# Batch 0's output product by fewer multiplications: four of its six row tiles as two pairs, and the work beside them in a new order

## The chip, the core and the metric

The kernel runs on one core of a Trainium2 chip. The core has a matrix engine (TensorE, in the profile PE, with its weight loads shown apart as PEld), a vector engine (VectorE, DVE), a scalar engine for functions and copies (ScalarE, ACT), GpSimd (POOL) and SyncE (SP); the last two issue DMA transfers here. The engines run beside each other and wait for each other through semaphores. Matrix products are summed in PSUM, a small memory of eight banks; all other tiles lie in SBUF. The metric is the device time of one execution in microseconds (us), as the median of several runs; smaller is better.

## The reference

An attention over 4 batches, 8 heads, 768 positions of 64 numbers is followed by a two-layer feed-forward block. A query sees the keys nearer than 16 positions, and for each block of 32 keys one summary: the maximum of the keys, the mean of the values.

```python
k_sum = k.reshape(B, H, nb, block, D).max(axis=3)
v_sum = v.reshape(B, H, nb, block, D).mean(axis=3)
scores_l = scale * np.matmul(q, k.transpose(0, 1, 3, 2))
mask_l = np.abs(pos[:, None] - pos[None, :]) < window
scores_s = scale * np.einsum('bhsd,bhnd->bhsn', q, k_sum) + np.log(block)
scores_all = np.concatenate([np.where(mask_l, scores_l, -1e9), scores_s], axis=-1)
a = softmax(scores_all)                      # the last axis
x = np.matmul(a, np.concatenate([v, v_sum], axis=2))
x = x.transpose(0, 2, 1, 3).reshape(B * S, H * D)     # 3072 x 512
h = x @ w_in                                 # 512 x 2048
out = (h / (1.0 + np.exp(-1.702 * h))) @ w_out        # 2048 x 512, f32
```

## The kernel before

Each batch has 768 tokens, worked on in two halves of 384. For each half the attention makes x, transposed, in `xTT`; the input stage (`ff_in`, `ff_open`, `ff_one`) multiplies it by `w_in` in 16 tiles of 128 features (four matmuls of 384 columns each) and ACT writes the activated result to `gTb`, which holds 16 feature tiles by 768 tokens. The output stage multiplies `gTb` by `w_out` into rows of 128 tokens, six per batch. The attention of the next half or batch runs beside the input and output stages of the one before.

The output product is done in one of two ways:

- plainly (`ff_out`, line 869): 16 matmuls of 512 columns for a row tile of 128 tokens, in four parts of four; then ACT copies the tile from PSUM and SP stores it;
- as a pair by seven products (`product`, line 775; Strassen's scheme in Winograd's form): the rows are a pair of token tiles, the features two halves of eight tiles, the columns two halves of 256. Seven products of eight matmuls of 256 columns replace two plain tiles. They take raw tiles of `gTb` and `w_out`, four sums of `gTb` (`gs`, by `g_sums` on DVE) and four differences of `w_out` (`ws`, by `w_sum`, each in two parts). Products 1, 6, 7 and 4 add up in one bank (A), 5 and 3 in another (B), 2 in a third (C). Between them the partial sum in A is saved to `s1` and `s2`, that in B to `s5`, by `keep_it`, and DVE adds them back in `give`; the next product must not write the bank before that copy has read it.

Batch 0 is worked plainly in two units of three tiles; batches 1 to 3 by seven products, with a tile of the first half paired with one of the second. The weight differences are made beside batch 0: four of the eight half differences after the first unit, four in the second unit's input stage.

What sets the order is written out by hand. Every engine runs its instructions in program order (`_Ordered`, line 18). `plan0`, `plan1` and `plan` (lines 1030 to 1038) say which piece of attention follows which block or product: "s" scores of a pair of heads (matmuls into PSUM, then an exponential on ACT), "m" its mask on DVE, "v" the values of two pairs (matmuls, then a reciprocal and a multiplication on DVE for each pair, the norm), "x" the turn of x on PE and its copy, "d" the same by DMA, "q" and "t" turns of queries, "g" a load of ACT's activation table. Two digits are half and pair (or group of two pairs), one digit the pair or group alone. `todo` (line 1102) lists the same for the second unit's input stage: `tk` turns a pair of keys, ACT copies it, DVE takes the block maxima, and POOL makes the halo and summary columns (`rest_k`, line 578). `value_rows` (line 1076) does the values' part: DMAs on SP that copy halo rows, 48 small matmuls that sum blocks (`vsum`, line 280), five DVE instructions that write the sums (`block_sums`), and two DMAs on SP that spread them.

PSUM is cut into two pools: `pmm` has four buffers of one bank, `psb` two buffers of two banks. Scores, values of batches 0, 2 and 3 and the turned x take `psb`; input tiles and output tiles take `pmm`. A new tile waits until some buffer's last reader is done.

POOL issues the loads of q, k and v, which also convert to 16 bits (`load_turned`, `load_v`: twelve loads for a batch's v). They are in POOL's program order together with its copies of keys; `load_batch(1)` stands at line 1027, `load_batch(2)` in the second output stage. For batch 3, waits on POOL (through `gate2`) hold back some loads until transposes by DMA have landed.

## Time and profile before

| | |
|---|---|
| median of 3 runs (range) | 206.83 us (205.51 to 206.84) |
| the profiled execution: time, span | 205.39 us, 203.4 us |
| PE busy, share of the span | 196.7 us, 97% |
| DVE busy | 141.2 us, 69% |
| ACT busy | 125.4 us, 62% |
| POOL busy | 89.9 us, 44% |
| first unit's output stage (batch 0) | from 30.66 us, 14.17 us long |
| second unit's input stage | from 44.83 us, 12.40 us long |
| block sums, then second unit's output stage | from 57.23 us, to 74.46 us |

The span runs from the first to the last record of the trace; the execution's time is longer by its start and end. The busy time of an engine other than PE counts where PE waits for it. Places in time are given from the span's start.

### The profile page before, as it was taken

Reading aid. Unit: us, or ns where it says so; the run is one execution under the profiler, and the core shown is the slowest. Engines: PE = TensorE matmul, PEld = TensorE weight load, DVE = VectorE, ACT = ScalarE, POOL = GpSimd, SP = SyncE. Lnnn points to the kernel's source line nnn. Section 1 sums busy time; section 2 is a strip of 40 time slices with the busy share of each in tenths; the row PEclk is TensorE's granted clock in tenths of the full one; section 3 lists DMA queues with packets and bytes.
Section 4 is the critical chain, followed back from the end, with each engine's and each line's share of the span. In section 5 each row is a group of like instructions: output and inputs, shape, how many; then the busy total and the mean of one; then the engine's idle time right before and its main releaser. Section 6 shows DMA issues by size and latency. Waiting matters only on the chain.

```text
span 203.4 us, 5851 instructions
## 1 busy us (share of the span) xinstructions
PE 196.7 (97%) x2358; PEld 136.6 (67%) x2358; DVE 141.2 (69%) x391; ACT 125.4 (62%) x240; POOL 89.9 (44%) x141
## 2 busy tenths in 40 slices
PE   6889999999999999999999999999999999999993
PEld 5548655556754566655888876666888865578882
DVE  6586894694856884898767789896769567758221
ACT  4584976638786717777871446778670559984220
POOL 7964489447899584000986034000000009980000
PEclk9999999999999999999999999999999999999999
DMA  5999999999999999999999979999022930000223
GB/s 171 169 165 204 207 207 215 189 156 243 116 122 170 176 170 178 127 165 155 114 181 156 173 140 139 110 247 179 0 104 62 185 119 3 0 0 0 106 105 103
DMA packets 95994, 28.13 MB, mean 138 GB/s; under 512 B 83664, under 2 KB 93152, under 8 KB 95968
## 3 DMA queue, kind: packets, MB, share of 16 engines
q0 software_dynamic: 69648, 13.24, 84.8%
q1 hardware_dynamic: 26176, 14.39, 34.8%
q8 instruction: 18, 0.29, 0.6%
q10 hardware_dynamic: 144, 0.13, 0.2%
q14 instruction: 8, 0.07, 0.1%
HBM read 27.26 MB, written 6.29 MB: 165 GB/s over the span
## 4 chain that ended last, share of the span: by engine, by line
PE 91%; DMA 3%; DVE 3%; issue 1%; ACT 0%; POOLq 0%; DVEq 0%
PE ph L28 32%; PE poA L28 16%; PE po L28 11%; PE poB L28 7%; PE phA L28 4%; PE ps_av L28 4%; PE poC L28 4%; PE ps_s L28 3%; DMA qe<-in_q_dram 3%; DVE ks L28 2%; PE ps_t L28 1%; PE ps_x L28 1%; PE phC L28 1%; PE phB L28 1%; PE phE L28 1%; DVE qT L28 1%
## 5 line engine op out<-in xcount | busy, mean ns | idle before, releaser
L28 PE MATMUL ph<-xT,w_in_sb 128*128 128x384 f16 x400 | 67.8, 326 | 0.1
L28 PEld LDWEIGHTS <-w_in_sb 128*128 128x128 f16 x442 | 42.7, 98 | 27.2 <-issue 0.2
L28 ACT ACTIVATE gT<-ph 128x384 f16<-128x384 f32 x100 | 47.9, 491 | 18.4 <-PE ph L28 17.6
L28 PEld LDWEIGHTS <-gT 128*128 128x128 f16 x312 | 28.8, 98 | 11.3 <-issue 0.2
L28 ACT ACTIVATE a_sb<-ps_s 128x768 bf16<-128x768 f32 (+1 forms) x32 | 25.0, 826 | 12.0 <-PE ps_s L28 12.0
L28 PEld LDWEIGHTS <-gs 128*128 128x128 f16 x288 | 27.7, 98 | 3.4
L28 POOL DMA_DIRECT2D vw<-in_v_dram x36 | 24.6, 699 | 11.9 <-DMA kb<-in_k_dram 5.4
L28 POOL TENSOR_TENSOR gs<-gT 128x384 f16<-128x384 f16 x8 | 7.3, 911 | 43.3 <-ACT gT L28 43.2
L28 PE MATMUL po<-w_out_sb,gT 128*128 128x512 f16 x96 | 23.6, 380 | 0.0
L28 PE MATMUL poA<-ws,gs 128*128 128x256 f16 x144 | 18.7, 273 | 0.0
L28 DVE TENSOR_TENSOR a_sb<-a_sb,mk 128x768 bf16<-128x768 bf16 x28 | 14.9, 554 | 5.5 <-ACT a_sb L28 5.0
L28 DVE TENSOR_TENSOR x<-ps_av,rc 128x384 f16<-128x384 f32 x32 | 17.8, 557 | 1.1
L28 DVE TENSOR_TENSOR gs<-gT 128x384 f16<-128x384 f16 (+1 forms) x34 | 13.3, 390 | 7.2 <-ACT gT L28 6.9
L28 POOL DMA_DIRECT2D qb<-in_q_dram x16 | 15.1, 961 | 2.5 <-DMA w_in_sb<-in_moe_w_in_dram 1.2
L28 PEld LDWEIGHTS <-kx 64*128 64x128 bf16 (+1 forms) x378 | 9.9, 95 | 6.8 <-issue 3.6
L28 POOL DMA_DIRECT2D kb<-in_k_dram x14 | 13.6, 986 | 0.3 <-issue 0.3
L28 DVE TENSOR_REDUCE ks<-kx 128x24 bf16<-128x768 bf16 x12 | 11.4, 948 | 3.4 <-ACT kx L28 3.2
L28 ACT ACT_TABLE_LOAD x10 | 12.8, 1283 | 1.0 <-PEq L1240 0.8
L28 ACT ACTIVATE osb<-poA 128x256 f32<-128x256 f32 x9 | 3.5, 384 | 16.1 <-PE poA L28 16.1
L28 ACT ACTIVATE s<-poA 128x256 f32<-128x256 f32 x11 | 4.2, 385 | 11.2 <-PE poA L28 11.2
L28 PEld LDWEIGHTS <-a_sb 128*64 128x64 bf16 (+2 forms) x400 | 7.9, 108 | 2.8 <-issue 1.3
L28 PE MATMUL poA<-ws,gT 128*128 128x256 f16 x72 | 9.3, 273 | 0.0
(117 smaller groups left out, 288.2 us busy)
## 6 DMA issues: line engine op xcount, KB each, us to landing
out_dram<-osb SPq DMA_DIRECT2D x22, 256.0 KB, 3.9
kb<-in_k_dram POOLq DMA_DIRECT2D x14, 192.0 KB, 6.6
qb<-in_q_dram POOLq DMA_DIRECT2D x12, 192.0 KB, 10.5
vw<-in_v_dram POOLq DMA_DIRECT2D x36, 64.0 KB, 5.5
w_out_sb<-in_moe_w_out_dram POOLq DMA_DIRECT2D x4, 512.0 KB, 12.8
w_in_sb<-in_moe_w_in_dram POOLq DMA_DIRECT2D x3, 512.0 KB, 12.4
vw<-vs SPq DMA_DIRECT2D x6, 198.0 KB, 6.6
gT<-in_k_dram SPq DMA_DIRECT2D x2, 384.0 KB, 3.4
```

The source lines that it names most:

```text
L28: r = f(*a, **kw)
```

## The change

Batch 0 is no longer two units of three plain tiles. The first two tiles of the first half are done plainly, and the other four (the first half's last tile and the three of the second half) are two pairs of neighbours, each by seven products, in the order `seq0`. `g_sums0` makes the four sums of `gTb` for them: the first four feature pairs in the second input stage, the other four beside the first products. All weight differences are therefore due by then: one moves into the first output stage (`"w0"`), seven follow it.

The attention beside these stages has new places. `plan0` now spreads batch 0's second half over eight blocks. `plan1` places batch 1's attention over fourteen products. In `values`, a mask can be put between the two norms of a group (`between`), and the values of batch 1 take `psb` but for the first group. The turned x of batches 0 and 1 is copied by ACT and not DVE, for batch 1 (but for the last two) from a `pmm` buffer; two query turns take `psb`. The block sums (`value_rows`) of batch 1 move from the end of the input stage to behind the first product, those of batches 2 and 3 from the second step of the input stage to the last, and always use `pmm`. `xq` of batch 3 moves from step 4 to step 2, and the block sums of batch 0 (`vrows0`) from the thirteenth input tile to the tenth.

Loads: of batch 1's v seven are issued first, the other five in two pieces between the key turns, and the second group of q after them (before, all v, then that group). Batch 2 loads k, q, v and not k, v, q. Batch 3 loads q with k and v after the gate (before, the other way round). The copy that saves `s1`, `s2` and `s5` of the first pair is ACT's for batch 0 and stays DVE's for batches 1 and 2.

```diff
@@ -129,12 +129,11 @@
                 pool.dma_start(out=t2[g][:, :, :, hh].rearrange("p i a d -> p (i a) d"),
                                in_=x[b, h0:h0 + 2].rearrange("h (a p) d -> p (h a) d", p=128))
-    def load_v(b):
+    def load_v(b, pieces=slice(0, 2 * NJ)):
         w5 = vw[b % 2].rearrange("p (j e) h c -> p j e h c", e=2)
         src = v[b].rearrange("h (j e p) d -> e j p h d", e=2, p=64)
-        for j in range(NJ):
-            for e in range(2):
-                pool.dma_start(out=w5[e * 64:e * 64 + 64, j, e, :, 0:D], in_=src[e, j])
+        for j, e in [(j, e) for j in range(NJ) for e in range(2)][pieces]:
+            pool.dma_start(out=w5[e * 64:e * 64 + 64, j, e, :, 0:D], in_=src[e, j])
     FAR = -30000.0
@@ -249,11 +248,9 @@
         load_turned(k, b, kb2, "kb")
         if b == 3:
             pool.tensor_copy(out=gate2, in_=qTs[0][:, NP - 1, 0:1])
+        load_turned(q, b, qb2, "qb", (0,) if b == 1 else (0, 1))
         if b == 1:
-            load_turned(q, b, qb2, "qb", (0,))
-        load_v(b)
-        if b < 3:
-            load_turned(q, b, qb2, "qb", (1,) if b == 1 else (0, 1))
+            load_v(b, slice(0, 7))
     def load_w_in(n0, n1):
         wi = moe_w_in.rearrange("(ko ki) n -> ki ko n", ki=128)
@@ -279,11 +276,7 @@
     def vsum(s):
-        if s == 1 and not vs_ps[0]:
-            ps = [pmm.tile([128, 512], F32, name="ps_vs", tag="mm") for e in range(2)]
-        else:
-            big = psb.tile([128, 1024], F32, name="ps_vs", tag="big")
-            ps = [big[:, 0:512], big[:, 512:1024]]
+        ps = [pmm.tile([128, 512], F32, name="ps_vs", tag="mm") for e in range(2)]
         vs_ps[0] = ps
         w5 = vw[s].rearrange("p (j e) h c -> p j e h c", e=2)
         for j in range(NJ):
...
@@ -598,9 +592,9 @@
         dve.tensor_mul(a, a, mk[:, half * TH:(half + 1) * TH, :].unsqueeze(1)
                        .to_broadcast([128, 2, TH, QT]))
-    def values(b, half, g):
-
-        if b == 1:
+    def values(b, half, g, mm=False, between=()):
+
+        if mm:
             banks = [pmm.tile([128, 512], F32, name="ps_av", tag="mm") for i in range(2)]
         else:
             ps = psb.tile([128, 1024], F32, name="ps_av", tag="big")
@@ -621,6 +615,8 @@
         x2[g] = attp.tile([128, 2, JH, 2, D], F16, name="x2", tag="x2", bufs=4)
         for i in range(2):
             norm(x2[g][:, :, :, i].rearrange("p h j d -> p j h d") if b else x2[g][:, i], pvs[i])
+            for f in between[i:i + 1]:
+                f()
     def norm(x, pv):
         rc = attp.tile([128, 2, JH, 1], F32, name="rc", tag="rc")
@@ -628,13 +624,13 @@
         dve.tensor_mul(x.rearrange("p j h d -> p h j d"), pv[..., 0:D],
                        rc.to_broadcast([128, 2, JH, D]))
-    def tx(half, g):
-        ps = psb.tile([128, 2, HALF], F16, name="ps_x", tag="big")
+    def tx(half, g, eng=dve, mm=False):
+        ps = (pmm if mm else psb).tile([128, 2, HALF], F16, name="ps_x", tag="mm" if mm else "big")
         for i in range(2):
             for j in range(JH):
                 pe.transpose(out=ps[:, i, j * 128:(j + 1) * 128],
                              in_=x2[g][:, i, j].rearrange("p h d -> p (h d)"), identity=ident16)
-        dve.tensor_copy(out=xTT[half][g], in_=ps)
+        copy(eng, xTT[half][g], ps)
     def dx(half, g):
         sp.dma_start(out=xTT[half][g].rearrange("p i (j c) -> p (i j) c", c=128),
@@ -688,6 +684,19 @@
             a, b_, op = {0: (a1[:, r], a2[:, r], ALU.add), 1: (gs[:, 0, j], a1[:, l], ALU.subtract),
                          2: (a1[:, l], a1[:, r], ALU.subtract), 3: (a2[:, l], gs[:, 1, j], ALU.subtract)}[w]
             eng.tensor_tensor(out=gs[:, w, j], in0=a, in1=b_, op=op)
+
+    def g_sums0(j0, j1, which, eng=dve):
+
+        def pairs(n0):
+            a = gTb[:, n0 + j0:n0 + j1, HALF - 128:S].rearrange("p j (a i c) -> p j a i c", i=2, c=128)
+            return a[:, :, :, 0], a[:, :, :, 1]
+
+        (l1, r1), (l2, r2) = pairs(0), pairs(NT // 2)
+        o = [gs[:, w, j0:j1, 0:256].rearrange("p j (a c) -> p j a c", c=128) for w in range(4)]
+        for w in which:
+            a, b_, op = {0: (r1, r2, ALU.add), 1: (o[0], l1, ALU.subtract),
+                         2: (l1, r1, ALU.subtract), 3: (l2, o[1], ALU.subtract)}[w]
+            eng.tensor_tensor(out=o[w], in0=a, in1=b_, op=op)
     N1 = d_model // 2
...
@@ -801,7 +810,7 @@
                 t_ = now[t, name] = spare[:, 2 * HALF + t * N1:2 * HALF + (t + 1) * N1]
             else:
                 t_ = now[t, name] = snap.tile([128, N1], F32, name=name, tag=name)
-            copy(dve if t == 0 and b + 1 < B else act, t_, po)
+            copy(dve if t == 0 and 0 < b and b + 1 < B else act, t_, po)
         def give(o, cols, name):
             if (t, o) not in now:
...
@@ -1027,11 +1039,12 @@
     load_batch(1)
-    plan0 = {1: ["q0", "q1", "q2"], 2: ["s0", "s1", "q3", "m0", "m1"], 4: ["s2", "s3", "m2", "m3"], 6: ["v0", "v1"], 8: ["x0"], 9: ["x1"]}
-
-    plan1 = {-1: ["s00", "s01"], 1: ["t2", "m00", "m01"], 2: ["t3", "s02"], 3: ["s03", "m02"], 4: ["m03", "s10"],
-             5: ["s11", "m10"], 6: ["v00", "m11", "s12", "s13"], 7: ["v01", "g"], 8: ["m12", "m13"],
-             9: ["x00", "x01", "v10"], 10: ["v11"], 11: ["x10"]}
+    plan0 = {0: ["q0", "q1"], 1: ["q2", "q3", "s0", "s1"], 3: ["s2", "s3", "m0", "m1", "w0", "m2", "v0"],
+             5: ["v1", "x0"], 7: ["x1"]}
+
+    plan1 = {0: ["R"], 2: ["s00", "s01"], 4: ["t2", "t3", "m00", "m01"], 5: ["s10", "s11"],
+             6: ["m10", "m11"], 7: ["s02", "s03"], 8: ["m02", "m03"], 9: ["s12", "s13"],
+             10: ["m12", "v00", "g"], 11: ["v01"], 12: ["x00", "v10"], 13: ["x01", "v11"]}
     plan = {-1: ["s00", "s01"], 2: ["m00", "m01"], 3: ["s02", "s03"], 5: ["m02", "m03", "s10", "s11"],
             7: ["m10", "m11", "s12", "s13"], 9: ["m12", "m13"], 10: ["v00", "v01"], 11: ["d00"],
@@ -1048,16 +1061,18 @@
                     gelu_soon()
             elif what[0] == "m":
                 mask(1, i)
+            elif what[0] == "w":
+                w_sum(0, 0)
             elif what[0] == "v":
-                values(0, 1, i)
+                values(0, 1, i, False, (lambda: mask(1, 3),) if i == 0 else ())
             else:
-                tx(1, i)
+                tx(1, i, act)
     def beside(b, slot):
         for what in (plan1 if b == 1 else plan).get(slot, ()):
             half, i = int(what[1:2] or 0), int(what[-1:] if len(what) > 1 else 0)
             if what[0] == "t":
-                tq(i, 1, dve)
+                tq(i, 1, dve, True)
             elif what[0] == "m":
                 mask(half, i)
             elif what[0] == "g":
...
@@ -1092,31 +1108,42 @@
     ws = keep.tile([128, 4, NT // 2, N1], F16, name="ws")
     exp_soon()
     beside0(-1)
-    for i, (ms, part) in enumerate((ms, part) for part in range(4) for ms in range(JH)):
+    for i, (ms, part) in enumerate((ms, part) for part in range(4) for ms in range(2)):
         ff_out(0, ms, part)
         beside0(i)
-        if i in (10, 11):
-            w_sum(i - 10, 0)
-            w_sum(i - 10, 1)
-
-    todo = {3: [lambda: tk(0, 1, act)], 4: [lambda: w_sum(2, 0)], 5: [lambda: tk(1, 1, act)],
-            6: [lambda: w_sum(2, 1)], 7: [lambda: w_sum(3, 0)], 8: [lambda: tk(2, 1, act)], 
-            10: [lambda: w_sum(3, 1)], 9: [lambda: tq(0, 1, dve)], 11: [lambda: tk(3, 1, act)], 12: [lambda: tq(1, 1, dve)],
-            15: [lambda: value_rows(1)]}
-    ff_in(1, range(3))
-    for nt in range(3, NT):
-        ff_in(1, (nt,))
-        for f in todo.get(nt, ()):
+    for what, part in ((0, 1), (1, 0), (1, 1), (2, 0), (2, 1), (3, 0), (3, 1)):
+        w_sum(what, part)
+
+    todo = {3: [lambda: tk(0, 1, act), lambda: load_v(1, slice(7, 9))],
+            5: [lambda: tk(1, 1, act), lambda: load_v(1, slice(9, 2 * NJ))],
+            8: [lambda: g_sums0(0, 4, (0, 1)), lambda: tk(2, 1, act)],
+            9: [lambda: tq(0, 1, dve), lambda: load_turned(q, 1, qb2, "qb", (1,)), lambda: g_sums0(0, 4, (2,))],
+            11: [lambda: tk(3, 1, act)],
+            12: [lambda: tq(1, 1, dve), lambda: g_sums0(0, 4, (3,))]}
+    ff_in(1, order2[0:4])
+    for f in todo[3]:
+        f()
+    for n in range(4, NT):
+        ff_in(1, (order2[n],))
+        for f in todo.get(n, ()):
             f()
     exp_soon()
-    beside(1, -1)
-    for i, (ms, part) in enumerate((ms, part) for ms in range(JH) for part in range(4)):
-        ff_out(1, ms, part)
+    for i, (t, what) in enumerate(seq0):
+        product(0, t, what)
+        if i == 0:
+            g_sums0(4, NT // 2, (0,))
+        if i == 1:
+            g_sums0(4, NT // 2, (2, 3))
         beside(1, i)
+        if i == 0:
+            g_sums0(4, NT // 2, (1,))
         if i == 2:
-            load_batch(2)
-        if i in (9, 11):
-            xk(i // 2 - 4, 0)
+            load_turned(k, 2, kb2, "kb")
+        if i == 4:
+            load_turned(q, 2, qb2, "qb")
+            load_v(2)
+        if i in (10, 12):
+            xk(i // 2 - 5, 0)
     halves[0] = True
@@ -1128,7 +1155,11 @@
                 win_sum(w)
         for n in range(0, NT, 2):
             if n == 0:
-                ff_open(order2[0:4], (lambda: tx(1, 1)) if b == 1 else None)
+                ff_open(order2[0:4], (lambda: tx(1, 0, act)) if b == 1 else None)
+                if b == 1:
+                    tx(1, 1)
+                    for nt in order2[4:6]:
+                        ff_one(0, nt)
             elif n == 2:
                 for nt in order2[0:4]:
                     ff_one(1, nt)
@@ -1136,16 +1167,16 @@
                 g_sums(1)
             else:
                 for nt in order2[n:n + 2]:
-                    for half in range(2):
+                    for half in range(int(b == 1 and n == 4), 2):
                         ff_one(half, nt)
                 g_sums(n // 2, dve, (0, 1) if n + 2 == NT else (0, 1, 2, 3))
             if nxt:
                 if n == 0 and b > 1:
                     pool.tensor_copy(out=gate2, in_=xTT[1][1][:, 1, 0:1])
-                    load_turned(q, b + 1, qb2, "qb")
-                if n // 2 == 1:
+                    load_v(b + 1)
+                if n // 2 == 7:
                     value_rows(s)
-                if n // 2 == 2 * b:
+                if n // 2 == 2:
                     xq(0, s)
                     xq(1, s)
                 if n // 2 in (2, 3, 4, 5):
```

Left out are the buffers of `tq` and the token rows that `product` reads and stores for a pair (for batch 0 the tiles at 256 and 384, or 512 and 640).

More of the change, by code (lines that the diff above doesn't have):

```diff
@@ L560, in tk, with tq @@
         rest_k(p, s, pool)
-    def tq(p, s, eng):
-        ps = pmm.tile([128, 1024], BF16, name="ps_t", tag="mm")[:, 0:S]
+    def tq(p, s, eng, big=False):
+        ps = (psb.tile([128, 2048], BF16, name="ps_t", tag="big") if big
+              else pmm.tile([128, 1024], BF16, name="ps_t", tag="mm"))[:, 0:S]
         turn_tiles(ps, qb2[p // 2][:, p % 2], NJ)
@@ L827, in product @@
             if last:
-                store("o1", t * 128, lo)
+                store("o1", tok_l, lo)
         elif what == 6:
@@ L1069, in beside @@
             elif what[0] == "v":
-                values(b, half, i)
+                first_ = b == 1 and half == i == 0
+                values(b, half, i, first_, (lambda: mask(1, 3),) if first_ else ())
             elif what[0] == "d":
@@ L1073, in beside @@
             else:
-                tx(half, i)
+                tx(half, i, act, True)
     def value_rows(s):
@@ L1085 @@
         ff_in(0, (nt,))
-        if nt == 12:
+        if nt == 9:
             act.activation(out=gate3[:, 0:1], in_=gate[:, 0:1], func=ACT.Copy)
```

14 lines of the change are left out of this document (8 added, 6 removed).

## The prediction

> **What bounds the kernel now.** The page's busy times come first, then its shares of the chain that ended last.
>
> ```profile
> PE 196.7 (97%) x2358; PEld 136.6 (67%) x2358; DVE 141.2 (69%) x391; ACT 125.4 (62%) x240; POOL 89.9 (44%) x141
> ...
> PE 91%; DMA 3%; DVE 3%; issue 1%; ACT 0%; POOLq 0%; DVEq 0%
> ```
>
> PE is on the chain nine tenths of the time. Who PE itself waited for, and for how long (total, times, longest):
>
> ```profile
> PE ps_h L28 <- DVE warm L28: 1.3, 1, 1.3
> PE ps_q L28 <- DMA qe<-in_q_dram: 0.8, 1, 0.8
> PE ps_b L28 <- DVE ks L28: 0.8, 2, 0.4
> PE ps_k L28 <- ACT kb L28: 0.5, 1, 0.5
> ```
>
> All of these belong to the opening attention. Three stages carry the change: the output stage of batch 0's first half (30.66 to 44.83), the input stage of its second half, and the second output stage with batch 1's attention. Columns are PE, weight loads, DVE, ACT, POOL, clock, DMA.
>
> ```profile
> 30.66:44.83 14.17, 14.17 (x183) 7.42 (x181) 9.16 (x21) 7.68 (x11) 9.18 (x12) 1.00 1.80 188
> 44.83:57.23 12.40, 12.40 (x108) 8.14 (x114) 8.40 (x13) 10.12 (x20) 9.67 (x21) 1.00 1.94 175
> 57.23:74.46 17.23, 17.23 (x316) 9.68 (x316) 12.40 (x32) 10.60 (x15) 14.03 (x23) 1.00 1.79 160
> ```
>
> PE is busy in every microsecond, at full clock. So a microsecond of matmul removed is a microsecond gained, and every wait that PE gets is lost in full. The question is how many waits the tighter order makes.
>
> **The change part by part.** *Matmuls.* The chain, in order of time (start, length):
>
> ```profile
> 30.66 1.73 PE po L28 x8
> 32.39 0.62 PE ps_q L28 x18
> 33.02 0.97 PE po L28 x4
> 33.98 0.46 PE ps_s L28 x24
> ...
> 57.23 0.53 PE ps_vs L28 x48
> ...
> 60.06 0.34 PE ps_t L28 x6
> ...
> 97.02 0.98 PE poA L28 x8
> 98.00 0.87 PE poB L28 x8
> ```
>
> Eight plain matmuls of 512 columns take 1.73, so a tile of sixteen takes 3.46; a product of eight matmuls of 256 columns takes 0.87 (0.1 more for either after scores or values, as often before as after). Four plain tiles go, 4 x 3.46 = 13.84; fourteen products come, 14 x 0.873 = 12.22. **Gain 1.62.** Scores, values, transposes and block sums stay the same in number; they only move.
>
> *First output stage, shorter by one tile.* The same attention must now go between eight blocks of four matmuls instead of twelve.
>
> ```profile
> 36.49 0.52 PE L28 MATMUL ps_s<-qT,kx 64*128 64x64 bf16 x24
> 36.88 1.51 ACT L28 ACTIVATE a_sb<-ps_s 128x768 bf16<-128x768 f32 x2 [1.00 <-PE ps_s L28]
> ```
>
> An exponential starts 0.39 after its scores start and takes 0.75. In the new order PE gets to s2 at 30.66 + 0.87 (block) + 0.41 (two query turns, two thirds of 0.62) + 0.97 + 0.41 + 0.46 (s0, s1) + 0.97 + 0.87 = 35.6, and s2 and s3 end at 36.06. The next thing in PE's order is v0, in a buffer of the pool of two that s2 and s3 have just filled. It is free when s2's exponential is over, 35.6 + 0.39 + 0.75 and some 0.1 of signalling, 36.85. **Cost 0.8** (0.6 to 0.9); before, four blocks lay between. Behind v0 all of PE is queued. v1, the turns and the input stage find their operands ready by my count: x1's copy by ACT behind two output copies ends near 43.2, and the second half of the four tiles needs it at 43.4. The stage ends at 44.83 - 3.46 + 0.8, about 42.1, and the input stage (12.40, the same PE work once the block sums are counted out) at 54.5.
>
> *DVE in the input stage.* It gets seven half weight differences at its start and four batch sums of 4 x 256 elements.
>
> ```profile
> L28 DVE TENSOR_TENSOR ws<-w_out_sb 128x1024 f16<-128x1024 f16 x4 | 2.6, 682 | 0.0
> L28 DVE TENSOR_TENSOR gs<-gT 128x384 f16<-128x384 f16 x33 | 11.7, 355 | 7.2 <-ACT gT L28 6.9
> ```
>
> The new g_sums0 has no row. By the first row (same size) one is 0.68, by the second, scaled by 1024/384, 0.95; I take 0.68, as the size is the same. Eight cost 5.5 to 7.6 on DVE. Seven differences from about 41, when v1's norms end, are over at 45.8, before the first key copy has ended on ACT (46.3), so the maxima, two query copies and sums follow with little queue and the last sum ends near 55.2. Hidden by the sixteen input tiles, at nothing; without that cover each slip is a slip of product 5.
>
> *Loads.* POOL issues the last five v loads between the key copies, and the second query group after them.
>
> ```profile
> 47.31 0.68 POOL L28 DMA_DIRECT2D vw<-in_v_dram  x1 [1.07 <-DMA qb<-in_q_dram]
> ...
> 52.56 2.04 POOL L28 DMA_DIRECT2D qb<-in_q_dram  x2
> 54.65 0.74 POOL L28 COPY kx<-kx 128x80 bf16<-128x80 bf16 x3
> 55.33 0.44 POOL L28 COPY kx<-ks 128x288 bf16<-128x288 bf16 x1
> ```
>
> Next, of the same trace's list of DMA issues, the time to landing (last column) of what was issued from 52 to 56:
>
> ```profile
> qb<-in_q_dram POOLq DMA_DIRECT2D x2, 192.0 KB, 5.3
> ...
> vw<-in_v_dram POOLq DMA_DIRECT2D x1, 64.0 KB, 3.1
> ```
>
> The seventh v load ends at 47.99 as before. One pair's key copies take 1.05 (54.65 to the next group's 55.70): 49.05; two v loads, 50.4; copies, 51.45; three v loads, 53.5, the last starting at 52.8 and landing at 55.9. Copies, 54.55; the query loads start at 54.55 and 55.6 and land 5.3 later, 59.9 and 60.9. The block sums come on PE after product 1, from 55.4 to 55.9, and their last eight matmuls read the twelfth v load: **cost 0.3** (0 to 0.6). The turn t2 of the third query pair is reached at 54.5 + 0.87 + 0.53 + 0.3 + 0.98 + 0.87 + 0.46 + 0.98 + 0.87 = 60.4 and needs both query loads: **cost 0.5** (0 to 1.3). Before, the same loads were issued 2.0 earlier and had landed when t2 came at 60.06. SP's halo copies and block-sum rows now stand at the head of this stage too; SP gets to the first store behind them near 59, and that store is not due before 64: nothing.
>
> *Products and attention mixed.* ACT now copies partial sums between exponentials.
>
> ```profile
> L28 ACT ACTIVATE s<-poA 128x256 f32<-128x256 f32 x11 | 4.2, 385 | 11.2 <-PE poA L28 11.2
> ```
>
> In slot 9 come s12 and s13, then product (1,6), then v00, then (1,7) in the same bank as (1,6), which ACT must first have saved. From the start of s12, PE needs 0.46 + 0.98 + 0.44 = 1.9; ACT needs 0.39 + 1.51 + 0.39 + 0.1 = 2.4. **Cost 0.5** (0 to 0.6). The same pattern in the first pair has two query turns in between and is covered.
>
> *Block sums late, batches 2 and 3.* They now stand after the last input tile; PE's 0.53 is the same, DVE's part moves.
>
> ```profile
> 57.94 0.29 DVE L28 COPY vpart<-ps_vs 128x128 f32<-128x128 f32 x1 [1.30 <-PE ps_vs L28]
> 58.27 1.18 DVE L28 TENSOR_TENSOR vs<-ps_vs,vpart 32x128 bf16<-32x128 f32 x4
> ...
> 97.12 0.36 DVE L28 TENSOR_TENSOR gs<-gT 128x384 f16<-128x384 f16 x1 [1.31 <-ACT gT L28]
> 97.52 0.36 DVE L28 TENSOR_TENSOR gs<-gs,gT 128x384 f16<-128x384 f16 x1
> 98.04 0.42 DVE L28 COPY s<-poA 128x256 f32<-128x256 f32 x1 [0.16 <-PE poA L28]
> ```
>
> Call the end of the input stage T (96.56 here). DVE does the two last sums until T + 1.3, then the copy and four adds of the block sums until T + 2.85, and only then the copy s that empties bank A, until T + 3.3. PE: block sums 0.53, scores 0.46, product 1 0.98, product 5 0.87 makes T + 2.84; product 6 must not write bank A before that copy. **Cost 0.5 a batch, 1.0 in all** (0 to 1.1). The block-sum rows land some 7 later, by T + 11, for the values at T + 12. The reordering of q before v for batch 3, and the earlier transposes of its queries, touch loads with 10 and more to spare: nothing, unless the v rows come after T, which would add their lateness.
>
> Sum: -1.62 + 0.8 + 0.3 + 0.5 + 0.5 + 1.0 = **+1.5**. With every uncertain wait at its lower end it is -1.0, at the upper end +2.9. The profiled execution took 205.39 (span 203.4 and 2.0 around it), the median of the runs shown is 206.83, and one of three runs is at 205.51. From the one the forecast is 206.9, from the other 208.3; I take the middle, **207.6**.
>
> **The rivals.** *The waits don't bite.* If buffers and copies come free earlier than my hand count (the counts are close: 0.5 here, 0.3 there), the gain of 1.62 stands but for some of the 0.8 of v0: 203.8 from the profiled run, 205.2 from the median, 204.5 in the middle. For it: PE had no wait in the middle of the kernel before, so the pattern has been easy to hide. Against: v0 follows its buffer's writer directly. Chance 0.15.
>
> *The second query group is late: slower.* It is the last of batch 1's loads. The page's median for such loads is far above what I took:
>
> ```profile
> qb<-in_q_dram POOLq DMA_DIRECT2D x12, 192.0 KB, 10.5
> ```
>
> At 10.5 the second lands at 66.1, t2 waits 5.7 instead of 0.5, and the time is 212.8; at 8 it is 210.3. It decides from a landing later than 60.4. Against: the 10.5 is from loads with a full queue ahead, here v and k are nearly through. [...] Chance of late queries, either way: 0.15.
>
> *DVE becomes the bound of the second output stage.*
>
> ```profile
> L28 DVE TENSOR_TENSOR a_sb<-a_sb,mk 128x768 bf16<-128x768 bf16 x28 | 14.9, 554 | 5.5 <-ACT a_sb L28 5.0
> L28 DVE TENSOR_TENSOR x<-ps_av,rc 128x384 f16<-128x384 f32 x32 | 17.8, 557 | 1.1
> L28 DVE RECIPROCAL rc<-ps_av 128x6 f32<-128x6 f32 x32 | 6.0, 188 | 2.9 <-PE ps_av L28 2.6
> L28 DVE TENSOR_TENSOR osb<-poA,s 128x256 f32<-128x256 f32 x9 | 3.8, 423 | 6.8 <-PE poA L28 6.8
> L28 DVE COPY qT<-ps_t 128x768 bf16<-128x768 bf16 x4 | 2.2, 551 | 1.0 <-PE ps_t L28 1.0
> ```
>
> Eight masks 4.4, eight norms of 0.7 5.6, six adds 2.5, two query copies 1.1, block sums 1.5, four batch sums 2.7: 17.8, against 12.40 in the window before and a stage of about 19 on PE. With sums at 0.95 it is 18.9. Any idle time on DVE then pushes the last norms behind the next input stage: +1 to +2 on the forecast, 209.1. For it: nearly full; against: the two last x turns have 1.3 of input tiles ahead of them. Chance 0.15.
>
> **How the numbers follow.** Forecast 0.55, no waits 0.15, late queries 0.15, DVE 0.15. One per cent, 2.1, is about what can be told from no change here: faster means below 204.8, slower above 208.9. Faster: two thirds of the first rival, 0.10. Slower: 0.13 of late queries, half of the DVE case and the upper tenth of the forecast's weight, 0.28. Within: 0.62. The range runs from 204.9 (most of the no-wait case) to 210.0 (the two slower cases but for the really late load).
>
> **What would show it.** Right: chain pieces of 0.87 for poA, poB and poC inside batch 0; PE waits for ACT a_sb at v0, for the last vw load, for qb at t2, for ACT s at (1,7), and DVE s twice after the input stages. Wrong: a PE list as short as now (no waits), POOL copies longer than 0.37 or qb landing after 61 (late queries), DVE without idle time from 55 to 74 (DVE). What would upset all of it is a buffer given out in another way than I assumed, so that PE waits for a bank at a place not named here.

## The result, and the profile after

The changed kernel takes 211.74 us (median of six runs, 209.62 to 214.27), the kernel before on the same chip 206.49 (six runs, 205.51 to 206.84). The ratio is 1.025, with a 95% interval from 1.021 to 1.030: 5 us slower, above the forecast of 207.6 and above its range. Here and below, a ratio is taken over the fast runs alone, without those that lie more than 1.5% above the quickest of their kernel. The runs show different granted clocks of TensorE: 209.62 us at 1.000, three runs of 211.20 to 212.16 at 0.990 to 0.992, and 212.98 and 214.27 at 0.982 and 0.983. The profiled execution is the quickest, 209.62 (span 207.6), against 205.39 before. So 4.2 of the loss can be seen in the traces. The rest, about 1, belongs to runs that were not profiled, and all five of them show a lower granted clock.

The page of the kernel after: busy times of the engines, and the engines' shares of the chain that ended last.

```profile
PE 195.4 (94%) x2406; PEld 141.6 (68%) x2406; DVE 146.5 (71%) x400; ACT 129.1 (62%) x249; POOL 91.0 (44%) x141
...
PE 63%; DMA 15%; POOL 13%; issue 4%; DVE 2%; ACT 1%; POOLq 0%
```

PE is busy for 1.3 us less than before (196.7): the products have saved what they were to save, nearly. But the chain now runs through DMA and POOL for 28% of the span, where before it was PE for 91%. What PE waited for (us in total, times, longest):

```profile
PE ps_t L28 <- DMA qb<-in_q_dram: 3.1, 1, 3.1
PE po L28 <- DMA w_out_sb<-in_moe_w_out_dram: 1.4, 1, 1.4
PE ps_h L28 <- DVE warm L28: 1.3, 1, 1.3
PE ps_b L28 <- DVE ks L28: 0.8, 2, 0.4
PE poA L28 <- DVE s L28: 0.8, 2, 0.4
PE ps_av L28 <- ACT a_sb L28: 0.7, 1, 0.7
PE ps_k L28 <- ACT kb L28: 0.6, 1, 0.6
PE poA L28 <- ACT s L28: 0.3, 1, 0.3
```

Five of these lines are new: the first two, the two with `poA`, and `ps_av`. They sum to 6.3. One line of before, 0.8 for `qe` at the opening, is missing. With 1.3 less of busy time on PE this makes 4.2, the measured difference of the two profiled executions.

The new waits in PE's timeline (start, length, instruction, in brackets the idle time before it):

```profile
34.37 1.89 PE L28 MATMUL po<-w_out_sb,gT 128*128 128x512 f16 x8 [1.45 <-DMA w_out_sb<-in_moe_w_out_dram]
...
37.44 0.64 PE L28 MATMUL ps_av<-vw,a_sb 128*64 128x65 bf16 x24 [0.73 <-ACT a_sb L28]
...
59.93 1.04 PE L28 MATMUL poA<-ws,gs 128*128 128x256 f16 x8
64.09 0.84 PE L28 MATMUL ps_t<-wide,qb 128*128 128x128 bf16 x12 [3.12 <-DMA qb<-in_q_dram]
...
72.62 1.03 PE L28 MATMUL poA<-ws,gs 128*128 128x256 f16 x8 [0.26 <-ACT s L28]
```

The large one stands at `t2`, the turn of batch 1's third query pair. It is reached at 60.97 and starts at 64.09. This is the place at which the prediction had put 0.5. POOL's own timeline shows what it did in the meantime:

```profile
52.25 2.04 POOL L28 DMA_DIRECT2D vw<-in_v_dram  x3
54.26 1.28 POOL L28 COPY kx<-kx 128x80 bf16<-128x80 bf16 x3
55.49 0.42 POOL L28 COPY kx<-ks 128x288 bf16<-128x288 bf16 x1
55.86 2.04 POOL L28 DMA_DIRECT2D qb<-in_q_dram  x2
...
58.55 0.91 POOL L28 COPY kx<-ks 128x288 bf16<-128x288 bf16 x1
```

The query loads are issued at 55.86, not at 54.55 as counted, and the list of DMA issues of the same trace gives their time to landing, 6.7 and not 5.3:

```profile
qb<-in_q_dram POOLq DMA_DIRECT2D x2, 192.0 KB, 6.7
```

That figure is the middle of the two loads, and t2 needs the second. Taken load by load, in the kernel before and then in the kernel after:

```profile
DMA to landing us min/median/max: 4.5/5.3/6.1
```

```profile
DMA to landing us min/median/max: 6.3/6.7/7.2
```

So the second load, issued at 56.88, landed at 64.1. In the kernel before, issued at 53.58, it landed at 59.7, only 0.2 ahead of t2 (59.89).

The two microseconds from 56 to 58, in the kernel before and then in the kernel after, show what the DMA engines did (columns: length, PE, weight loads, DVE, ACT, POOL busy, clock, DMA share, GB/s):

```profile
56.00:58.00 2.00, 2.00 (x76) 1.29 (x76) 0.70 (x3) 1.66 (x4) 2.00 (x8) 1.00 1.85 200
```

```profile
56.00:58.00 2.00, 2.00 (x62) 1.66 (x61) 1.82 (x5) 1.63 (x3) 2.00 (x3) 1.00 0.24 22
```

Before, 200 GB/s: the query loads, issued from 52.56 on, are under way. After, 22: POOL copied keys until 55.86 and is only now issuing them, so the engines that bring them have almost nothing to do.

### The profile page after: what moved, and what is told of

It is laid out like the page before. It is cut to its first block, busy times and chain, and to the rows that moved or that the text cites. A ratio compares the mean times of both kernels' runs of the same rounds, so it can differ in the third digit from the quotient of the medians.

```text
span 207.6 us, 5961 instructions
## 1 busy us (share of the span) xinstructions
PE 195.4 (94%) x2406; PEld 141.6 (68%) x2406; DVE 146.5 (71%) x400; ACT 129.1 (62%) x249; POOL 91.0 (44%) x141
## 4 chain that ended last, share of the span: by engine, by line
PE 63%; DMA 15%; POOL 13%; issue 4%; DVE 2%; ACT 1%; POOLq 0%
PE ph L28 21%; PE poA L28 17%; PE poB L28 8%; DMA w_in_sb<-in_moe_w_in_dram 6%; DMA kb<-in_k_dram 6%; PE phA L28 4%; PE poC L28 4%; DMA qb<-in_q_dram 3%; PE ps_av L28 2%; POOL vw L28 2%; POOL mk L28 2%; POOL v0n L28 2%; POOL kb L28 2%; PE ps_s L28 2%; POOL kx L28 2%
## 5 line engine op out<-in xcount | busy, mean ns | idle before, releaser
L28 PEld LDWEIGHTS <-gs 128*128 128x128 f16 x352 | 33.7, 98 | 5.6 <-issue 1.4
L28 PEld LDWEIGHTS <-gT 128*128 128x128 f16 x296 | 27.9, 98 | 8.1 <-issue 1.4
L28 PE MATMUL poA<-ws,gs 128*128 128x256 f16 x176 | 22.9, 273 | 1.1 <-DVE s L28 0.8
L28 DVE TENSOR_TENSOR gs<-gT 128x384 f16<-128x384 f16 (+2 forms) x38 | 16.3, 430 | 8.1 <-ACT gT L28 7.7
L28 ACT ACTIVATE osb<-poA 128x256 f32<-128x256 f32 x11 | 4.2, 384 | 17.0 <-PE poA L28 17.0
L28 ACT ACTIVATE s<-poA 128x256 f32<-128x256 f32 x15 | 5.8, 385 | 11.4 <-PE poA L28 11.4
L28 PE MATMUL poA<-w_out_sb,gT 128*128 128x256 f16 x88 | 11.5, 273 | 0.0
L28 PE MATMUL poA<-ws,gT 128*128 128x256 f16 x88 | 11.4, 273 | 0.0
L28 PE MATMUL poB<-w_out_sb,gs 128*128 128x256 f16 x88 | 11.4, 273 | 0.0
```

The costliest lines, as they stand in the source:

```text
L28: r = f(*a, **kw)
```

## The experiments

Each ratio is to the kernel before on the same chip in the same hour; its median there was 205.74 us for r1 to r4, 205.94 for r6 to r9 and 206.18 for r10 to r12.

**Who is late when the queries are not?** r1_q_before_v loads the second query group ahead of the last three v pieces, and puts batch 1's block sums a little later.

```diff
-5: [..., lambda: load_v(1, slice(9, 2 * NJ))],
+5: [..., lambda: load_turned(q, 1, qb2, "qb", (1,)), lambda: load_v(1, slice(9, 2 * NJ))],
-9: [..., lambda: load_turned(q, 1, qb2, "qb", (1,)), ...],
+9: [..., ...],
-plan1 = {0: ["R"], 2: ["s00", "s01"],
+plan1 = {2: ["s00", "s01", "R"],
```

> The changed kernel, but batch 1's second query group is loaded before the last three v loads, and the block sums of batch 1 stand behind the first scores instead of behind the first product. Theory (POOL issues that group too late, and PE's wait for it is most of the loss): the group is issued near 52.3 instead of 55.9, lands near 59, and PE's wait at t2 (3.1 to 3.4 us) falls under 0.5; the wait for the last v load may be 0.3; the median goes from 211.7 to 206 to 208, and the spread of the runs shrinks. Rival (the DMA engines are the limit, and the order of issue only decides who is late): the v rows are late in its place, the block sums wait 2 to 3 us, and the time stays within 1 us of 211.7.

Measured: 210.29 us, ratio 1.022 (1.015 to 1.030). The query loads are issued at 52.46, the wait at t2 is gone from the list of waits, and this line stands at its head instead:

```profile
PE ps_av L28 <- DMA vw<-vs: 2.4, 3, 1.6
```

Two of the three waits, 2.0 in all, are batch 1's: its rows of block sums now arrive late, as the rival said, though the time is 1.4 below the kernel after's. How much of this comes from the order of the loads is not shown. The edit itself put the block sums later (on PE they start at 58.42 instead of 56.13), and behind that they waited only 0.4 for the last v loads.

**The clock.** In r2_fill PE fills the wait with sixty needless turns whose result is overwritten.

```diff
+        if big and p == 2:
+            for i in range(60):
+                pe.transpose(out=ps[:, 0:128], in_=ident, identity=ident)
         turn_tiles(ps, qb2[p // 2][:, p % 2], NJ)
```

> The changed kernel with sixty needless transposes of the identity (128 x 128, overwritten at once by the turn itself) ahead of the turn t2, where PE waits for the query load. Theory (the time above the profiled 209.6, up to 214, is a lower matrix clock after PE's long idle time): with PE busy through the wait the wait costs the same, 3.3 us, but the granted clock stays at 1.00 in every run, the median falls from 211.7 to 209.0 to 210.0, and the runs lie within 1 us. Rival (the spread has another cause, such as the landing of the load): the median stays at 211 to 212 and the spread at 4 us.

Measured: 211.31 us (210.17 to 213.06), ratio 1.027 (1.020 to 1.034). All four granted clocks are 0.999 or 1.000, but the time has not fallen. In the profiled execution, the slowest, the queries took 9.1 to land:

```profile
qb<-in_q_dram POOLq DMA_DIRECT2D x2, 192.0 KB, 9.1
```

and t2 still waited 2.69 behind the sixty turns. So, as far as four runs can show it, the lower clock comes from PE's idle time, but the clock alone does not keep the time up: at full clock it is as long. The landing time differs too, 6.7 against 9.1 for the same two loads, and at full clock the runs still lie 2.9 apart. Why this kernel is no quicker stays open.

**The block sums of batches 2 and 3, alone.** r3_sums_early makes them one step earlier, in the pool of wide buffers.

```diff
-                if n // 2 == 7:
-                    value_rows(s)
+                if n // 2 == 6:
+                    value_rows(s, True)
```

> The changed kernel with the block sums of batches 2 and 3 one step earlier (after the seventh of eight steps of the input stage, in the two-bank pool), so that DVE is through with them before the last sums. Theory: the two waits of product 6 for DVE's copy s (0.4 each) go, and the time falls by 0.8, to about 211 in the median, less than its spread can show; in the profile no wait of poA for DVE s. Rival (the wait only moves to another place of the output stage): those two waits go but the stage from the input stage's end to the next one keeps its length.

Measured: 211.63 us (209.01 to 212.91), ratio 1.024 (1.016 to 1.032). In the trace both waits of product 6 are gone, and the time from batch 1's first input tile to batch 2's is 44.78 (78.24 to 123.02) against 45.23 (77.92 to 123.15) after; from batch 2's to batch 3's it is 44.01 against 44.45. That is the 0.4 a batch that the prediction had put there. In the median it can't be seen, because the t2 wait, 3.4 here, varies by more.

**Both, with v0 in another buffer.** r4_three joins r1 and r3 and gives v0 two single banks.

```diff
-values(0, 1, i, False, (lambda: mask(1, 3),) if i == 0 else ())
+values(0, 1, i, i == 0, (lambda: mask(1, 3),) if i == 0 else ())
```

> Three edits together: the second query group before the last three v loads with batch 1's block sums behind the first scores, the block sums of batches 2 and 3 one step earlier, and the first values of the first output stage in the one-bank pool so that they need not wait for an exponential. Theory (the waits add up): -3.3, -0.8, -0.7 on the profiled 209.6 gives 204.8 to 205.5, about 1 us below the kernel before, whose median is 206.5. Rival (PE that comes earlier meets the next late transfer: the second quarter of w_out in the first stage, the v rows in the third): 206 to 207.5.

Measured: 210.68 us, ratio 1.024 (1.018 to 1.030), above what the theory and the rival had said. The rows of block sums of batch 1 are late again (2.5), the last v loads cost 1.1, and v0, free of its buffer, waits as long for something else:

```profile
37.40 0.54 PE L28 MATMUL ps_av<-vw,a_sb 128*64 128x65 bf16 x23 [0.82 <-DMA vw<-vs]
...
75.82 1.89 PE L28 MATMUL poB<-w_out_sb,gs 128*128 128x256 f16 x8
```

The second row is a product of eight matmuls some 2.6 behind the longest wait (1.99, at 73.19): 1.89 where it is 1.05 otherwise. The mean granted clock from 74 to 78 is 0.57, and 1.00 in the stretches before and after.

**The load order of batch 1, alone, in the kernel before.** r9_before_loads_between changes nothing else: TensorE keeps its old order.

```diff
-        load_v(b)
-        if b < 3:
-            load_turned(q, b, qb2, "qb", (1,) if b == 1 else (0, 1))
+        load_v(b, slice(0, 7) if b == 1 else slice(0, 2 * NJ))
+        if b in (0, 2):
+            load_turned(q, b, qb2, "qb", (0, 1))
...
-    todo = {3: [lambda: tk(0, 1, act)], ... 5: [lambda: tk(1, 1, act)], ... 9: [lambda: tq(0, 1, dve)], ...
+    todo = {3: [lambda: tk(0, 1, act), lambda: load_v(1, slice(7, 9))], ...
+            5: [lambda: tk(1, 1, act), lambda: load_v(1, slice(9, 2 * NJ))], ...
+            9: [lambda: tq(0, 1, dve), lambda: load_turned(q, 1, qb2, "qb", (1,))], ...
```

> One part of the change alone, in the kernel before: batch 1's loads go between the key copies as in the kernel after (seven v pieces, copies of the first pair, two v pieces, copies, three v pieces, copies, second query group); TensorE keeps the order of before. Theory (the interleaved loads are enough to make the query group late): the query loads are issued near 54.9 to 55.9, land near 62 to 63.5, and t2, at 59.9 in the kernel before, waits 2 to 3.5; the last v pieces land later as well, and the block sums at 57.2 may wait up to 0.5. The time is 208.5 to 211.5. Rival (the load order costs nothing by itself, the loss comes from TensorE's new order with the block sums behind it): within 0.5 of the kernel before, 205.5 to 206.5.

Measured: 212.57 us (212.04 to 213.09), ratio 1.032 (1.029 to 1.036), no less than the whole change costs. The rival is out. The issue of the query loads, the wait at t2, and the stretches around it (the clock is the third number from the end):

```profile
56.50 2.03 POOL L28 DMA_DIRECT2D qb<-in_q_dram  x2
```

```profile
PE ps_t L28 <- DMA qb<-in_q_dram: 4.6, 1, 4.6
```

```profile
60.00:66.00 6.00, 1.39 (x10) 0.84 (x9) 0.35 (x1) 0.74 (x2) 6.00 (x8) 0.92 1.94 168
66.00:70.00 4.00, 4.00 (x40) 1.98 (x38) 2.35 (x5) 1.35 (x3) 1.04 (x2) 0.70 2.94 155
```

The wait costs 4.6, and behind it the clock falls: 6 x 0.08 + 4 x 0.30 = 1.7 us of TensorE lost. With 0.4 by which this execution was late already when it came to t2 (4.97 later than before, of which 4.61 are the wait), the sum is 6.7, and the spans differ by 6.6 (210.0 and 203.4). My expectation (up to 211.5) left the clock out.

**The load order of batch 1, undone, in the kernel after** (r6_loads_first).

```diff
-            load_v(b, slice(0, 7))
+            load_v(b)
+            load_turned(q, b, qb2, "qb", (1,))
...
-todo = {3: [..., lambda: load_v(1, slice(7, 9))], 5: [..., lambda: load_v(1, slice(9, 2 * NJ))], ...
-        9: [..., lambda: load_turned(q, 1, qb2, "qb", (1,)), ...], ...
+todo = {3: [...], 5: [...], ... 9: [..., ...], ...
```

> One part of the change undone: batch 1's loads are issued in one run as in the kernel before (keys, first query group, all twelve v pieces, second query group), and POOL's key copies follow behind them; the order of TensorE is that of the kernel after. Theory (the query group is late because POOL does key copies between the loads, so that they are issued later and the DMA engines run dry between them): POOL issues the query loads near 52.6, they land by 58 to 59, ahead of the place of t2 near 60.9, and the wait of 3.1 to 3.4 us at t2 is gone. The median loses those 3 us and what followed from the long idle time, and is 206 to 207.5, as the kernel before within 1%. Rival (the new order of TensorE leaves too little time for batch 1's loads, in whatever order they are issued): the wait moves to keys, block-sum rows or v pieces, POOL's key copies, now behind all loads, hold up s00 or s10, and the time stays at 209 or more.

Measured: 207.65 us (207.02 to 208.51), ratio 1.008 (1.005 to 1.012), clocks 0.998 to 1.000. The queries are issued at 52.79, and t2 starts at 60.33 without a wait:

```profile
52.79 2.07 POOL L28 DMA_DIRECT2D qb<-in_q_dram  x2
```

```profile
60.33 0.84 PE L28 MATMUL ps_t<-wide,qb 128*128 128x128 bf16 x12
```

Most of the loss is gone. Not all of it, for two lines are new:

```profile
PE ps_vs L28 <- DMA vw<-in_v_dram: 1.4, 4, 0.5
...
PE ps_av L28 <- DMA vw<-vs: 0.9, 1, 0.9
```

They are of batch 2: its block sums wait for v (from 95.54), and its values wait for the rows made from them. POOL's timeline has the reason:

```profile
65.00 4.07 POOL L28 DMA_DIRECT2D qb<-in_q_dram  x4
69.00 1.44 POOL L28 DMA_DIRECT2D vw<-in_v_dram  x2
...
79.54 0.68 POOL L28 DMA_DIRECT2D vw<-in_v_dram  x1 [4.95 <-DMA qb<-in_q_dram]
```

The change loads batch 2's queries ahead of its v, and the v loads stand behind them in POOL's order. In the kernel after this cost nothing: the last v load landed at 96.6 and the block sums came only at 99.43, since PE had lost 3 us at t2 and more ahead of it. Here they come at 95.54, 3.9 sooner, and would have waited for a landing at 96.6 too: one wait covered the other. Part of the wait is new, for the last v load lands at 98.1 here. Batch 2's loads start 1.6 later (60.99 against 59.41), behind all of batch 1's key copies.

**The same, with the block sums one step earlier** (r7_loads_first_sums: the edit of r3_sums_early on top).

> The same as r6_loads_first, and the block sums of batches 2 and 3 one step earlier, in the wide pool (as in r3_sums_early). Theory: the two waits of product 6 for the copy s (0.41 each) go as well: 0.8 to 0.9 below r6_loads_first, 205.2 to 206.5, level with or a little under the kernel before. Rival (the two gains overlap, or the earlier block sums meet v rows that land later in this order): no more than 0.2 below r6_loads_first.

Measured: 210.26 us, ratio 1.018 (1.014 to 1.022): worse by 2.6, not better. The rival holds, and by more than it said. Sums that come earlier meet the same late v:

```profile
95.93 0.25 PE L28 MATMUL ps_vs<-vw,E 64*32 64x128 bf16 x7 [1.90 <-DMA vw<-in_v_dram]
```

and the clock falls to 0.72 from 96 to 102, another 6 x 0.28 = 1.7.

**Batch 2's v ahead of its queries**, as in the kernel before, on top of r6_loads_first (r10_v2_first).

```diff
-            load_turned(q, 2, qb2, "qb")
-            load_v(2)
+            load_v(2)
+            load_turned(q, 2, qb2, "qb")
```

> r6_loads_first, and batch 2's v pieces issued before its queries, as in the kernel before. In r6_loads_first the block sums of batch 2 wait for v pieces 1.4 us in four stretches (95.5 to 98.4), since eight query loads stand ahead of them in POOL's queue. Theory (those waits come from the order of the loads alone): the v pieces are issued by 76 and land by 80, the four waits go, the queries are still turned in time for step 2, and the time falls 1.2 to 1.6 below r6_loads_first, to 206.0 to 206.6. Rival (the queries come late instead, as the last of a long queue): a wait of 1 us or more for query or key tiles in batch 2, and no gain.

Measured: 206.04 us (205.53 to 207.35, eleven runs), ratio 1.001 (0.998 to 1.004). The four waits are gone, and the queries are not late. What is left in the list beside the opening:

```profile
PE poA L28 <- DVE s L28: 0.8, 2, 0.4
PE ps_av L28 <- ACT a_sb L28: 0.7, 1, 0.7
PE po L28 <- DMA w_out_sb<-in_moe_w_out_dram: 0.7, 1, 0.7
...
PE poA L28 <- ACT s L28: 0.3, 1, 0.3
```

These sum to 2.5, against 1.5 less of busy time on PE and 0.8 of before's opening wait that this execution does not have. What is left of the change, the fewer matmuls and the new order of the engines, neither gains nor costs anything that can be told.

**And the block sums earlier, on top of that** (r11_v2_first_sums).

> r10_v2_first, and the block sums of batches 2 and 3 one step earlier, as in r7_loads_first_sums, where that alone made things worse because the v pieces were late (1.9 us and more). Theory: with the v pieces there, only the gain of r3_sums_early is left, 0.4 a batch: 0.6 to 0.9 below r10_v2_first, 205.2 to 206.0, the kernel before's own time within 0.5. Rival (the earlier sums wait for something else): level with r10_v2_first or above it.

Measured: 205.40 us (median of twelve runs), ratio 0.997 (0.994 to 0.999): a little under the kernel before, and the lowest median of all kernels here. The waits of product 6 are gone from the list. By the medians that is worth 0.6, near the 0.8 of the two waits; the intervals of r10 and r11 still overlap a little.

**v0 a block later, on top of that** (r12_v0_later).

```diff
-3: [..., "w0", "m2", "v0"], 5: ["v1", "x0"], 7: ["x1"]}
+3: [..., "w0", "m2"], 4: ["v0"], 5: ["v1"], 6: ["x0"], 7: ["x1"]}
```

> r11_v2_first_sums, and in the first output stage the values v0 one block of four matmuls later, v1 behind the next one and the turn x0 behind the one after that. Theory (v0's wait of 0.73 is only for s2's exponential to free the buffer): a block of 0.87 covers it, the wait is gone, x0 still finds its norms ready, and the time is 0.5 to 0.7 below r11_v2_first_sums, 204.5 to 205.5. Rival (the norms of v0 and v1 on DVE are what is late behind it): the wait moves to x0 or x1 or to the first input tiles of the second half, and nothing is gained.

Measured: 205.75 us (twelve runs), ratio 0.998 (0.996 to 1.001), no gain over r11_v2_first_sums. The wait of v0 is gone, and PE runs into `w_out` instead, whose quarters have not landed:

```profile
33.88 1.89 PE L28 MATMUL po<-w_out_sb,gT 128*128 128x512 f16 x8 [0.44 <-DMA w_out_sb<-in_moe_w_out_dram]
...
37.12 1.02 PE L28 MATMUL po<-w_out_sb,gT 128*128 128x512 f16 x4 [0.90 <-DMA w_out_sb<-in_moe_w_out_dram]
```

Neither the theory nor the rival had this. With one tile fewer in the first output stage, a quarter of `w_out` serves two blocks and not three, so the next is due sooner; the waits of 0.44 and 0.90 stand at the first block of the second quarter and of the third.

**POOL beside DVE's sums.** In the kernel after, the third pair's three copies took 1.28 while a batch sum ran on DVE (54.66 to 55.34); in the kernel before, where no sum ran beside them, 0.74. r8_sum_moved is the kernel after, with this sum two steps earlier.

```diff
+            10: [lambda: g_sums0(0, 4, (3,))],
-            12: [lambda: tq(1, 1, dve), lambda: g_sums0(0, 4, (3,))]}
+            12: [lambda: tq(1, 1, dve)]}
```

> The kernel after, with its fourth batch sum (o1 - l2 side, the one at 54.66 in its trace) two steps earlier, from behind the thirteenth input tile to behind the eleventh, where POOL issues loads and copies nothing. [...]

Measured: 211.07 us (median of four runs, 208.88 to 213.92); the ratio, 1.017 (1.012 to 1.022), rests on two of them. It can't be told clearly from the kernel after. POOL's timeline:

```profile
51.90 0.89 POOL L28 COPY kx<-ks 128x288 bf16<-128x288 bf16 x1
52.74 2.04 POOL L28 DMA_DIRECT2D vw<-in_v_dram  x3
54.75 0.76 POOL L28 COPY kx<-kx 128x80 bf16<-128x80 bf16 x3
55.43 0.44 POOL L28 COPY kx<-ks 128x288 bf16<-128x288 bf16 x1
55.81 2.03 POOL L28 DMA_DIRECT2D qb<-in_q_dram  x2
```

The third pair's copies take 0.76, where they took 1.28. But now the second pair's last copy has two sums beside it on DVE, one from 51.71 to 52.50 and the moved one from 52.43 to 53.34: the copy takes 0.89 where it took 0.42, the moved sum 0.91 where it took 0.68. The delay is one pair earlier, so the query loads start at 55.81 as in the kernel after, and t2 waits no less (3.74, landing 6.9). Here as in the kernel after, POOL's copies ahead of these loads take 0.5 us more beside a sum. No run shows why.

## Why the prediction was wrong

**The step that failed** is the loads: "the query loads start at 54.55 and 55.6 and land 5.3 later, 59.9 and 60.9 ... cost 0.5 (0 to 1.3)". Measured in the profiled execution, the quickest: the second load was issued 1.3 later (56.88) and took 1.9 longer to land (7.2), PE came to t2 0.6 later (60.97), and so the wait cost 3.1. Four things were missing in it.

- *POOL's time.* I took each group of key copies at its undisturbed 1.05. The third took 0.54 more: its first three copies 1.28 for 0.74, while a batch sum ran on DVE; with that sum moved (r8_sum_moved) they took 0.76. And the three v loads ahead of it began at 52.25, not 51.45, as one of the two before them had waited 0.64 for an earlier load. The forecast's sum has no term for either.
- *The second load.* The 5.3 is the middle of the two loads of before; the second, on which t2 depends, took 6.1 there. With that figure the forecast's own issue at 55.6 gives a landing at 61.7 and a wait of 1.3, the upper end of its range. It also hid that the kernel before had only 0.2 to spare here, so that nearly every delay of these loads is lost in full.
- *The queue.* I took the landing of 5.3 from a trace in which the loads follow each other without a gap. With copies between them the DMA engines run empty (22 GB/s against 200). The queries then come when the halo copies and the next batch's keys (issued from 59.41) use the same engines, at 168 GB/s, and the second takes 1.1 longer than before (7.2 against 6.1); the middle of the two is 6.4 in r9_before_loads_between and 9.1 in r2_fill. In the kernel before they had landed by 59.7, soon after the next keys were issued at 58.86. That this company makes the landing longer is argued from these rows; no run separates it.
- *The clock.* A wait of PE was priced at its own length. In some executions 1.7 us more is lost behind it at a lower clock, and no line of the prediction has that. The kernel after's runs at 0.990 to 0.992 lie 1.6 to 2.5 above the profiled one. But r2_fill keeps its clock and is hardly quicker, so how much of the way from 209.62 to 211.74 is the clock, and how much later landings, stays open.

The late query group was a rival, with 210.3 for a landing after 8 us, at a chance of 0.15. I gave it so little because "v and k are nearly through" by then. That speaks of the queue's length; what mattered was when the loads entered it. Its landing after 8 us stood for 63.6, and the second load landed at 64.1: about the right size, but reached in part through the later issue. That the load order was the cause is shown from both sides: alone in the kernel before it costs 6.6 us (ratio 1.032), and undone in the kernel after it gives back 3.5 to 4 (ratio 1.025 to 1.008, median 211.74 to 207.65).

**A second miss, hidden by the first.** The prediction took up the order of queries and v for batch 3 and not for batch 2. There q before v costs 1.6 us (207.65 to 206.04) once the t2 wait no longer covers it.

**The other terms, by their measured size.**

| step | predicted | measured |
|---|---|---|
| matmuls saved | 1.62 | 0.7 to 1.5 (PE busy 196.7; after 195.4, r10 195.2, r12 196.0) |
| v0 behind s2's exponential | 0.8 | 0.73 |
| block sums wait for the last v load | 0.3 | nothing in the list (0.6 in r3, 0.5 in r8) |
| (1,7) behind ACT's copy | 0.5 | 0.26 |
| product 6 behind the copy s, batches 2 and 3 | 1.0 | 0.8 |
| second quarter of `w_out` | not seen | 0 to 1.45 |
| first batch sum on DVE | 0.68 | 0.69 |

The hand count of the waits for PE, ACT and DVE was good to 0.3 in each place. Without the term of the queries the forecast's sum is +1.0; with both load orders undone it measures 0.0 (ratio 1.001). `w_out` was overlooked since the trace of before shows no wait for it. In the profiled execution after, PE also got to it about a microsecond sooner, as the opening wait for `qe` was absent. That is not the whole reason, for r11 lacks the opening wait as well and does not wait for `w_out`. How much of 1.45 is lost in a usual execution stays open; it is 0.7 in r10 and nothing in r11.

The DVE rival fell: the sums ended where the count had them (the fourth from 54.66 to 55.34), and DVE stood idle for 3.8 in the t2 wait. In r6_loads_first, without that wait, it was still idle for 4.25 of the 21.5 us from 54.5 to 76. The rival that no wait bites fell too, but with its order of loads mended and the sums moved, the change reaches 205.4, a ratio just under one.

## What to carry to other kernels

When a change puts an engine's own work between the transfers that it issues, price the last transfer by when it can enter the queue and by what runs then, not by the landing time in a trace where the queue was kept full. Price a long wait of TensorE with the clock that it can cost afterwards, 1.7 us in each of the three traces of which the sum is given here. And when undoing one cause returns less than its wait, look for the next wait that it had covered.

## What the runs showed of the hardware

- After an idle stretch of PE the granted clock can fall for a few microseconds. Behind a wait of 4.6 us it is 0.92 on average from 60 to 66 and 0.70 from 66 to 70 (r9_before_loads_between); behind one of 2.0 it is 0.57 from 74 to 78, where a product takes 1.89 against 1.05 (r4_three); and with a string of waits from 94 to 98, of which the longest is 1.9, it is 0.72 from 96 to 102 (r7_loads_first_sums). In each of the three 1.7 us are lost (4 x 0.43 in r4_three), and the run's mean clock is 0.992; by the same sum a run at 0.982 has lost about 3.8 (0.018 x 212, an estimate, as none was profiled). It is not certain: the profiled executions with waits of 3.1 (after) and 3.4 (r3_sums_early) kept 1.000. Nor is a long wait at t2 the only occasion: two of 29 runs of the kernel before, measured beside r10 to r12, show 0.992 and one of the twelve of r11 0.991, and no trace of these was kept.
- Two loads of 192 KB from the same queue landed, in the middle of the two, after 5.1 us (r10_v2_first), 5.8 (r6_loads_first), 6.7 (after) and 9.1 (r2_fill), and no run separates what made the difference. In the slower two the first was issued at 55.86 and 55.55, and the next batch's keys from 59.41 and 59.16; in r6_loads_first these stand at 52.79 and 60.99.
- Where a POOL copy and a batch sum on DVE ran at the same time in these traces, one of them or both took longer than apart. In the kernel after the copies of 80 columns took 1.28 for three, against 0.74, with the sum at 0.68; a copy of 288 columns beside a sum that began 0.15 after it kept its 0.42, with the sum at 0.83 against 0.69; another took 0.91, with the sum at 0.77. In r8_sum_moved one took 0.89, and the moved sum 0.91.
